# A 4 KB transfer of the first chunk's rows, issued on the ScalarE queue ahead of everything else

## The chip, the core and the metric

The kernel runs on one core of a Trainium2 chip. The metric is the device time of one execution in microseconds, the median of several executions. The profile is of one execution; its span is the time from the core's first to its last instruction.

## What is computed

The input is q, k and v, each of 4 batches, 8 heads, 768 positions and 64 dimensions. Per head there is a retention with a decay of its own, and then a gated feed-forward part over the joined heads:

```python
state = gamma * state + k[t] (outer) v[t]        # per head, 64 x 64
y[t]  = scale * q[t] @ state
x = y with the heads joined: 4 x 768 x 512
h = maximum(x @ w_in, 0)                          # 1024 wide
conv_out = a 3-tap convolution of h along the positions, with conv_w per channel
out = (h * sigmoid(conv_out)) @ w_out             # 512 wide
```

## The kernel before

The retention goes in 24 chunks of 64 positions for two batches at a time. The program on the host has laid q, k (transposed), k and v of one chunk beside each other: `qkv[n]` is 128 rows of 4 slots of 512 floats, so 8 KB a row and 1 MB a chunk. For the first four chunks one load brings slots 0 and 1 (`load`, L348, 4 KB of each row, 512 KB) and a second one slots 2 and 3 (`load_kv`, L352); later chunks come with one load of 1 MB.

The feed-forward part goes in 12 units of 2 x 128 positions. `w_in` and `w_out` arrive as 8-byte numbers, a piece of 512 KB at a time (`load_w`, L476), and VectorE and ScalarE turn each piece into a head and a rest in fp32r (`w_abs` L494 to `w_add` L575). The first product (`mm1`, L589) has the heads and rests of `w_in` (`wi_hi`, `wi_lo`) as the weights of TensorE and `xu` as the moving operand, 256 columns at a time. For six of the units there are combined products (`prod`, L710); some of these use `wi_hi` and `wi_lo` too. The second product (`mm2`, L807) has the gated activations `g` as weights and the converted `w_out`, kept in tiles `h`, as moving operand: 512 columns, and 256 columns for the last tile.

All instructions are given in an order written out by hand (`ORDER`), and every engine works through its own in that order. The beginning is

```
load_w/0 load_w/1 load/0 load_consts load_kv/0 load_w/2 load/1 load_kv/1 load_gy load/2 w_abs/0 ...
... w_head/0 w_clamp/1 w_rest/0 scores/0 w_low/0 masked/0 scale_v/0 w_add/0 w_shift/1 w_abs/2 mix/0
```

All loads are issued on SyncE's queue. TensorE begins with 6 products of zeros (`fill`, L329; each is two passes in the profile), then does `scores/0` (L409), which needs `load/0`, then three more products of zeros (`keep_warm`, L323), and then `mix/0`, which needs the masked scores (`masked`, L436, VectorE) and the scaled v of chunk 0 (`scale_v`, L377, ScalarE, after `load_kv/0`). `load_kv/2` is held back until `mix/0` has been issued.

The SBUF tiles come from two pools, laid out in the order in which the tiles are named. The pool `const` holds 1,664 bytes a partition of constants, then `gy_sb`, `cw_sb`, `wi_hi` (16,384 bytes), a gap of 128, `wi_lo` (16,384), a gap of 128, and, as they are first used, `first` (one float, which takes 32 bytes), `cw_t` (192) and `cw_m` (96). Behind it follows `pool`, whose first tiles are set down by name and size, and then `o_sb` and the chunks `rw`:

```
g_0:4096 g_1:4096 g_2:4096 g_3:4096 h_7:2048 h_8:2048 h_a:2048 h_b:2048 h_e:2048
h_g:2048 h_h:2048 h_k:2048 h_m:2048 h_n:2048 h_q:2048 h_s:2048 h_t:2048 h_1:2080
h_0:2080 h_p:2080 h_3:2080 h_5:2080 h_6:2080 h_j:2080 h_9:2080 h_2:2080 h_c:2080
h_r:2080 h_d:2080 h_f:2080 h_i:2080 h_l:2080 h_o:2080 h_4:2080 h_u:2080 h_v:2080 gap0:32
xu_0:8192 xu_1:8192 xu_2:8192 x_0:2048 ... x_c:2048 m_0:2048 ... cv_2:2048 gap1:64
```

Each DMA counts on one of eight semaphores, taken in turn; a DMA that takes one again waits for the DMA that had it before.

Of the kernel before, what the change touches and what calls it, by code (L numbers as in the profile page):

```python
# [9 lines left out]
F32 = mybir.dt.float32  # L10
# [8 lines left out]
P = 128  # L19
# [244 lines left out]
def retention_then_gated_ffn(  # L264
# [10 lines left out]
    nc = tc.nc  # L275
# [6 lines left out]
    const = ctx.enter_context(tc.tile_pool(name="const", bufs=1))  # L282
# [27 lines left out]
    for i, place_ in enumerate(PLACES.split()):  # L310
        name, size = place_.split(":")
        pool.tile([P, int(size) // 4], F32, name=name, bufs=1)

    warm = pool.tile([P, P], F32, name="o_sb", bufs=2)
    nc.vector.memset(warm, 0.0)
# [570 lines left out]
```

## Time and profile before

| | |
|---|---|
| median of 3 runs | 332.17 us (331.81 to 334.49) |
| the profiled execution | 331.37 us |
| its span | 329.6 us |
| TensorE busy | 319.8 us, 97% of the span |
| VectorE, ScalarE, GpSimd busy | 288.4, 214.8 and 25.7 us |
| read from HBM, written | 33.79 MB, 6.29 MB |
| chain that ended last | TensorE 86%, DMA 6%, VectorE 4% |

The profiled execution took 0.80 us less than the median, and 1.8 us of it lie outside its span. An engine's rows give the start and the duration of an instruction, in microseconds from the start of the span; the bracket behind a row is the idle time of the engine ahead of it and what ended that. A DMA's row is its issue; when its data is there is seen from who starts then.

### The profile page before, as it was taken

To read this page: it belongs to the slowest core of one execution; us is meant where nothing else is said; L and a number is where in the kernel's file an instruction comes from. 1 tells how busy PE (TensorE), PEld (TensorE's weight loads), DVE (VectorE), ACT (ScalarE), POOL (GpSimd) and SP (SyncE) were. 2 spreads that over 40 slices of the span, in tenths; PEclk is the share of its full clock that TensorE was granted. 3 is DMA by queue.
4 is the path that set the end of the run, shared out by engine and by line. 5 is a ranking of instruction groups with operands and counts; after the bars stand their busy time and mean duration, and the time that the engine had idled before them with its cause. 6 is when DMAs were issued, how large, how long until landed. Compare 5 with 4: busy or idle time off the path is not lost.

```text
span 329.6 us, 10762 instructions
## 1 busy us (share of the span) xinstructions
PE 319.8 (97%) x4642; PEld 285.9 (87%) x4642; DVE 288.4 (87%) x566; ACT 214.8 (65%) x448; POOL 25.7 (8%) x100
## 2 busy tenths in 40 slices
PE   8789999999999999999999999999999999999996
PEld 3678999999998988788888998999999888988785
DVE  4699999999999999996999998788988887879980
ACT  4567675747466484855848755976696866676761
POOL 0000002003020200200000000021002200120000
PEclk9999999999999999999999999999999999999999
DMA  6999687736435312463260000000000101010111
GB/s 227 373 337 362 223 286 284 252 133 231 179 132 230 130 57 107 161 233 110 111 195 34 34 0 33 36 0 2 32 34 0 64 2 65 3 64 0 66 64 64
DMA packets 10415, 40.77 MB, mean 124 GB/s; under 512 B 1280, under 2 KB 1792, under 8 KB 7808
## 3 DMA queue, kind: packets, MB, share of 16 engines
q1 hardware_dynamic: 10368, 40.09, 33.6%
q8 instruction: 36, 0.59, 0.7%
q14 instruction: 11, 0.09, 0.1%
HBM read 33.79 MB, written 6.29 MB: 122 GB/s over the span
## 4 chain that ended last, share of the span: by engine, by line
PE 86%; DMA 6%; DVE 4%; ACT 1%; issue 1%; SPq 0%; ACTq 0%
PE ps_o L807 39%; PE ps_m L589 17%; PE ps_m L710 8%; PE ps_y L710 7%; DMA rw<-in_qkv 6%; PE ps_s L409 5%; PE ps_st L409 4%; PE ps_y L409 3%; PE ps_s L710 2%; DVE cv L772 1%; ACT cv L778 1%; PE ps_o L323 0%; DVE cv L783 0%; DVE rw L436 0%; DVE m L512 0%
## 5 line engine op out<-in xcount | busy, mean ns | idle before, releaser
L589 PE MATMUL ps_m<-xu,wi_hi 128*128 128x256 f32 x384 | 68.2, 281 | 0.6 <-ACT h_o L601 0.5
L807 PE MATMUL ps_o<-h,g 128*128 128x512 f32 (+1 forms) x200 | 62.3, 381 | 0.0
L589 PEld LDWEIGHTS ps_m<-xu,wi_hi 128*128 128x128 f32 x384 | 58.0, 188 | 1.9 <-ACT h_o L601 0.7
L589 PE MATMUL ps_m<-xu,wi_lo 128*128 128x256 f32 x192 | 53.2, 277 | 0.0
L778 ACT ACTIVATE cv<-cv 128x512 f32<-128x512 f32 x48 | 29.9, 630 | 34.3 <-DVE cv L772 34.3
L409 PE MATMUL ps_y<-rw 64*64 64x64 f32 x1472 | 48.5, 220 | 0.8 <-issue 0.8
L409 PEld LDWEIGHTS ps_y<-rw 64*64 64x64 f32 x1472 | 45.2, 135 | 1.4 <-issue 0.9
L807 PEld LDWEIGHTS ps_o<-h,g 128*128 128x128 f32 x200 | 37.2, 188 | 6.7 <-ACT o_sb L814 0.2
L772 DVE SCALAR_TENSOR_TENSOR cv<-h,cw_sb,cv 128x256 f32<-128x256 f32 x84 | 38.7, 478 | 1.0 <-ACT cv L767 0.3
L793 DVE TENSOR_TENSOR g<-cv,g 128x512 fp32r<-128x512 f32 x48 | 32.6, 686 | 6.7 <-ACT g L788 6.3
L788 ACT CAST g<-cv 128x512 fp32r<-128x512 f32 x48 | 29.3, 616 | 12.1 <-DVE cv L783 11.0
L589 PEld LDWEIGHTS ps_m<-xu,wi_lo 128*128 128x128 f32 x192 | 36.0, 188 | 0.0
L409 PEld LDWEIGHTS ps_s<-rw 64*64 64x64 f32 x768 | 24.6, 134 | 9.0 <-issue 3.6
L409 PE MATMUL ps_s<-rw 64*64 64x64 f32 x768 | 28.0, 221 | 3.9 <-DMA rw<-in_qkv 1.9
L409 PE MATMUL ps_st<-rw 64*64 64x64 f32 x704 | 24.9, 219 | 0.5 <-ACT rw L377 0.5
L377 ACT ACTIVATE rw<-rw,consts_sb 128x128 f32<-128x128 f32 x64 | 20.4, 390 | 6.4 <-DMA rw<-in_qkv 6.4
L409 PEld LDWEIGHTS ps_st<-rw 64*64 64x64 f32 x704 | 22.6, 135 | 1.5 <-ACT rw L377 0.9
L436 DVE TENSOR_TENSOR rw<-ps_s,consts_sb 128x512 f32<-128x512 f32 x24 | 16.4, 685 | 6.5 <-PE ps_s L409 6.5
L767 ACT ACTIVATE cv<-h,cw_sb 128x256 f32<-128x256 f32 x42 | 20.5, 503 | 2.0 <-DVE g L793 2.0
L814 ACT COPY o_sb<-ps_o 128x512 f32<-128x512 f32 (+1 forms) x25 | 13.9, 560 | 10.1 <-PE ps_o L807 10.0
L807 PE MATMUL ps_o<-h_g,g 128*128 128x512 f32 (+1 forms) x50 | 19.3, 387 | 0.0
L807 PE MATMUL ps_o<-h_s,g 128*128 128x512 f32 (+1 forms) x50 | 19.2, 385 | 0.0
(256 smaller groups left out, 754.6 us busy)
## 6 DMA issues: line engine op xcount, KB each, us to landing
rw<-in_qkv SPq DMA_DIRECT2D x20, 1024.0 KB, 6.0
out_y<-o_sb SPq DMA_DIRECT2D x23, 256.0 KB, 2.2
g<-in_w_in SPq DMA_DIRECT2D x8, 512.0 KB, 5.4
rw<-in_qkv SPq DMA_DIRECT2D x8, 512.0 KB, 7.9
g<-in_w_out SPq DMA_DIRECT2D x8, 512.0 KB, 4.8
out_y<-o_sb SPq DMA_DIRECT2D x2, 128.0 KB, 1.7
consts_sb<-in_consts SPq DMA_DIRECT2D x1, 128.0 KB, 10.2
consts_sb<-in_consts SPq DMA_DIRECT2D x1, 80.0 KB, 7.3
```

Of the source, the lines that this page charges most:

```text
L377: nc.scalar.activation(v[:, :, g], v[:, :, g], AF.Copy, scale=by[:, g : g + 1])
L409: nc.tensor.matmul(out, lhsT, rhs, start=start, stop=stop, skip_group_check=True)
L436: nc.vector.tensor_tensor(out=rw[n][:, 1], in0=s_ps[n], in1=mask_sb.unsqueeze(1).broadcast_to([P, 2, NPAIR, C]), op=ALU.mult)
L589: nc.tensor.matmul(h_ps[u, p][:, odd], w[:, k, fs], x[:, k].rearrange("p b t -> p (b t)"), start=(i == 0), stop=(i == len(products) - 1),)
L710: nc.tensor.matmul(ps[:, i], w[k][:, fs], x[:, k].rearrange("p b t -> p (b t)"), start=(i == m == 0 and q in (1, 5)), stop=(m == len(produ ...
L767: nc.scalar.activation(cvs[u, p][:, i], hs[u, p][:, i, :, 1 : P + 1], AF.Copy, scale=cw_sb[:, f, 1:2])
L772: nc.vector.scalar_tensor_tensor(out=cv, in0=h[:, :, k : k + P], scalar=cw_sb[:, f, k : k + 1], in1=cv, op0=ALU.mult, op1=ALU.add)
L778: nc.scalar.activation(cvs[u, p], cvs[u, p], AF.Sigmoid)
L788: nc.scalar.copy(gs[u, p][:, 0], cvs[u, p])
L793: nc.vector.tensor_tensor(out=lo, in0=cvs[u, p], in1=hi.bitcast(F32), op=ALU.subtract)
L807: nc.tensor.matmul(ps, g, w[f][:, cs], start=(f == 0 and i == 0), stop=(f == NF - 1 and i == 2))
L814: nc.scalar.copy(o[:, :n], o_ps[u, t, h][:, :n])
```

## The change

A tile of 8 floats a partition is added to the pool `const`, ahead of `first`, and ScalarE's first instruction becomes a DMA that brings the first 32 bytes of each of the 128 rows of chunk 0 into it. Nobody reads the tile.

```diff
@@ -311,6 +311,10 @@
         name, size = place_.split(":")
         pool.tile([P, int(size) // 4], F32, name=name, bufs=1)
 
+
+    ahead = const.tile([P, 1, 8], F32, name="ahead")
+    nc.scalar.dma_start(ahead, qkv[0][:, :1, :8])
+
     warm = pool.tile([P, P], F32, name="o_sb", bufs=2)
     nc.vector.memset(warm, 0.0)
     first = const.tile([P, 1], F32, name="first")
```

## Rows read from the trace of the kernel before

**Rows 1.** Page, part 1: busy time of each engine, its share, its instructions.

```profile
PE 319.8 (97%) x4642; PEld 285.9 (87%) x4642; DVE 288.4 (87%) x566; ACT 214.8 (65%) x448; POOL 25.7 (8%) x100
```

**Rows 2.** Chain that ended last, its first 19 us: start, duration, what.

```profile
1.65 7.57 DMA rw<-in_qkv
...
9.25 1.15 PE ps_s L409 x32
10.40 1.49 PE ps_o L323 x6
...
13.07 5.56 DMA rw<-in_qkv
```

**Rows 3.** Windows: length, busy time by engine, clock, DMA share, GB/s.

```profile
2.50:4.50 2.00, 2.00 (x3) 0.67 (x2) 0.00 (x0) 0.47 (x1) 0.00 (x0) 1.00 1.01 403
4.50:7.50 3.00, 3.00 (x8) 1.43 (x7) 2.67 (x6) 1.50 (x3) 0.00 (x0) 1.00 0.78 207
9.00:12.00 3.00, 2.75 (x48) 2.25 (x52) 1.55 (x3) 1.19 (x4) 0.00 (x0) 1.00 1.02 417
14.00:18.00 4.00, 2.77 (x100) 2.28 (x97) 3.43 (x6) 2.51 (x7) 0.00 (x0) 1.00 0.93 314
```

**Rows 4.** Timeline of the first 14 us: ScalarE and SyncE's queue (SPq).

```profile
0.73 1.28 ACT L317 ACT_TABLE_LOAD   x1 [0.73 <-PEq L875]
...
0.74 0.86 SPq L476 DMA_DIRECT2D g<-in_w_in  x2
...
2.03 0.20 ACT L317 ACTIVATE first<-o_sb 128x1 f32<-128x1 f32 x1
...
4.03 0.66 ACT L494 ACTIVATE m<-g 128x512 f32<-128x512 f32 x1 [1.80 <-DMA g<-in_w_in]
4.05 0.58 SPq L352 DMA_DIRECT2D rw<-in_qkv  x1
...
5.31 0.69 ACT L494 ACTIVATE m<-g 128x512 f32<-128x512 f32 x1 [0.61 <-DMA g<-in_w_in]
...
10.81 1.28 ACT L377 ACTIVATE rw<-rw,consts_sb 128x128 f32<-128x128 f32 x4 [3.81 <-DMA rw<-in_qkv]
```

**Rows 5.** Timeline of the first 15 us: TensorE and VectorE.

```profile
1.05 7.27 PE L329 MATMUL ps_o<-o_sb 128*128 128x512 f32 x12 [1.05 <-DVE o_sb L315]
...
7.66 0.68 DVE L528 SCALAR_TENSOR_TENSOR g<-g 128x512 f32<-128x512 uint32 x1
...
10.45 0.69 DVE L436 TENSOR_TENSOR rw<-ps_s,consts_sb 128x512 f32<-128x512 f32 x1 [2.11 <-PE ps_s L409]
...
14.61 0.69 DVE L436 TENSOR_TENSOR rw<-ps_s,consts_sb 128x512 f32<-128x512 f32 x1 [0.57 <-PE ps_s L409]
```

**Rows 6.** DMA issues: KB of each, median microseconds from issue to landing.

```profile
rw<-in_qkv SPq DMA_DIRECT2D x8, 512.0 KB, 7.9
```

**Rows 7.** Groups of TensorE's instructions by form: count, busy, mean ns, idle before.

```profile
L589 PE MATMUL ps_m<-xu,wi_hi 128*128 128x256 f32 x384 | 68.2, 281 | 0.6 <-ACT h_o L601 0.5
...
L589 PE MATMUL ps_m<-xu,wi_lo 128*128 128x256 f32 x192 | 53.2, 277 | 0.0
...
L710 PE MATMUL ps_m<-xu,wi_hi 128*128 128x256 f32 x48 | 8.7, 281 | 0.0
...
L710 PE MATMUL ps_m<-xu,wi_lo 128*128 128x256 f32 x24 | 6.6, 276 | 0.0
```

**Rows 8.** Timeline of TensorE in two stretches: 211 to 215 us, and 324 to 326 us.

```profile
211.07 0.39 PE L710 MATMUL ps_m<-xu,wi_hi 128*128 128x256 f32 x2
...
213.80 0.39 PE L807 MATMUL ps_o<-h,g 128*128 128x512 f32 x1
...
215.17 1.53 PE L710 MATMUL ps_y<-xu,rw 128*128 128x256 f32 x12
...
324.02 0.28 PE L807 MATMUL ps_o<-h_b,g 128*128 128x256 f32 x1
...
325.94 0.28 PE L807 MATMUL ps_o<-h_s,g 128*128 128x256 f32 x1
```

## The prediction

> **What bounds the kernel now.** First the page: TensorE is busy 97% of the span [rows 1], so a gain has to begin in TensorE's idle time or shorten its instructions. The chain of waits says where the idle time is: of its first 19 us 7.57 + 5.56 = 13.13 are two DMAs of `qkv` [rows 2], the first of them `load/0`, issued at 1.65 and followed at 9.25 by `scores/0`. The change touches this one.
>
> The windows show why `load/0` is late. The queue works in order: `load_w/0`, `load_w/1`, `load/0`. The two pieces of `w_in` flow at 403 GB/s and are there when ScalarE starts on them, at 4.03 and 5.31 [rows 3, 4]: 1.28 us for 512 KB. The next 512 KB are `load/0` [rows 6], and they would be there at 5.31 + 1.28 = 6.6. They land at 1.65 + 7.57 = 9.22, since between 4.5 and 7.5 us only 207 GB/s flow, with the DMA engines 78% busy [rows 3]. From 9 to 12 us, where the same queue brings chunk 1 from the neighbouring megabyte among other things, it is 417 GB/s again. The transfer added reads rows of chunk 0 before its turn; if the slow stretch belongs to the first reading of that memory, some of it could pass while `w_in` flows.
>
> **What late data costs.** Not all of the 2.6 us can come back. The products of zeros end at 1.05 + 7.27 = 8.32 [rows 5], and `scores/0` stands behind them: it can start 9.25 - 8.32 = 0.93 us earlier and no more. Then TensorE goes on without idle time into `keep_warm` and `mix/0` (9.25 + 1.15 = 10.40, + 1.49 = 11.89 [rows 2]), so 0.93 is the cap there too, if the v of chunk 0 is scaled in time: ScalarE waits for `load_kv/0` until 10.81 [rows 4], and that transfer stands behind `load/0` and moves with it. `load_kv/2`, held by `mix/0` and issued at 13.07, moves as well. VectorE is idle for 2.11 us ahead of the first `masked`, and 0.57 us ahead of the second, at 14.61 [rows 5]; from there on to the end of the 30 us its row of instructions has no idle time that the timeline marks. So what the start can give in all is 0.93, or 0.93 + 0.57 = 1.50 if that second hole closes too.
>
> **The change part by part.**
>
> *The issue on ScalarE.* The trace has no DMA issue on that engine. SyncE's cost 0.43 (0.86 for two) to 0.58 [rows 4], and I take 0.5. ScalarE's table load and the first activation end at 2.03 + 0.20 = 2.23; they would end at 2.73. The next instruction waits for `load_w/0` until 4.03 [rows 4]. Cover 1.80, cost on the path nothing; without the cover 0.5.
>
> *The packets.* 128 rows of 32 bytes, 4 KB. From below the time is that of 4 KB at 403 GB/s, 0.01 us; from above that of a transfer with as many rows of 4 KB, 1.28 [rows 4]. It is nearer to the lower end by bytes, and I take 0.1. If all of the 1.28 were put ahead of `load_w/0`, VectorE's conversions, which end at 7.66 + 0.68 = 8.34 [rows 5], would end at 9.6, and `load/0` without its slow stretch would land at 6.6 + 1.28 = 7.9, still before 8.32. So this too is covered where the transfer helps; where it doesn't, `scores/0` is late by 0.1, at most 1.28.
>
> *The semaphore.* The new DMA takes the first of the eight, so the ninth, `load_kv/1`, has to wait for it. SyncE issues that at 4.05 [rows 4], by when `load_w/0`, issued beside the new one, has landed (4.03). Behind it are `load_gy` and `load/2`. Cost nothing; all other pairs that share a semaphore keep their distance of eight.
>
> *The gain.* Between 0 and 0.93. For a gain: chunk 1 is read without a slow stretch, so rows, size and pitch alone don't make one. Against: the windows of 14 to 18 us, with `load/2` and `load_kv/2`, flow at 314 GB/s with the engines 93% busy [rows 3], so reading `qkv` is slowed elsewhere too, by something that 32 bytes a row may not take away. I take the middle, 0.5.
>
> The Trainium skill, in its page HBM Reference, section Latency, gives 0.2 us for an access on average and 2 us under high load. By that rule load makes reading slow, and the touch would gain nothing: 332.2 instead of 331.7. The trace disagrees: the higher rate goes with the faster stretch [rows 3].
>
> *The 32 bytes.* The tile `ahead` stands in the pool `const` behind `wi_hi` and `wi_lo` and moves all of `pool` up by 32 bytes a partition. The weights of L589 and of some of L710 stay, and their moving operand moves. By the sizes in the code `xu` begins 33,344 (`wi_hi` to the end of `const`) + 16,384 (`g`) + 26,624 + 39,520 (`h`) + 32 = 115,904 bytes above `wi_hi`, 192 past a multiple of 256, and 64 past one above `wi_lo`; with the change 224 and 96. Does this matter? Two stretches of products with 256 columns differ: 24 of L710 take 213.80 - 211.07 = 2.73 us, 114 ns each, and 16 of L807 take 325.94 - 324.02 = 1.92, 120 ns each [rows 8]. In L807 weights `g` and moving `h` are a multiple of 256 apart. With 512 columns L807 takes (215.17 - 213.80) / 6 = 228 ns [rows 8], so there nothing is seen of it. That the distance is the cause is my reading. Distances of 224 and 96 have no row: 114 ns is one bound, 120 the other. From below no row of 256 columns is faster than 114, and I leave a small chance that one would be. The products concerned are 384 + 192 of L589 and three times 48 + 24 of L710 (the two rows shown and two pairs alike) [rows 7], 792 in all; times 6.2 ns that is 0 to 4.9 us, nearly all on the path with TensorE 97% busy. I take 0, the row of the same instructions, and keep the other end for the range.
>
> **The sum.** 331.37 - 0.5 = 330.9 for the profiled execution, which was 0.80 below the median; on the scale of the median 332.17 - 0.5 = 331.7.
>
> **The rivals.**
>
> *Slower: the products with `wi_hi` and `wi_lo` lose their distance.* For it: the 120 against 114 ns, and 792 products on the engine that is the bound. Against: with a distance between the two seen, part or none of it may come. Half gives 331.7 + 2.5 = 334.2, all 336.6. It decides from 0.5 / 792 = 0.6 ns a product upwards, and is over 1% from (335.5 - 331.7) / 792 = 4.8 ns, a pace of 119.
>
> *The touch doesn't do what it is for.* The slow stretch stays: rows are slow one by one, or because 16 engines read `qkv` in step. Then 332.2, and up to 332.3 with the packets in the way. For it the 314 GB/s at 14 to 18 us, against it the 417 at 9 to 12 [rows 3].
>
> *More than the cap at `scores/0`.* If the second hole of VectorE closes too: 332.17 - 1.5 = 330.7. Against it: VectorE has no idle time to give back afterwards.
>
> **How the numbers follow.** The forecast, a gain of 0 to 0.93 with the pace unchanged, 331.2 to 332.2: 0.42. The slower pace: 0.33, of which 0.13 over 335.5. The touch without effect: 0.17. The larger gain: 0.05. A faster pace: 0.03. The range goes from 330.4, the larger gain with 0.3 for the runs' own scatter (332.17 - 331.81 = 0.36), to 335.5, where 0.13 is left out above and some 0.04 below. One per cent, 3.3 us, is about what a measurement of this kernel can tell from no change. Over 1% faster needs the faster pace: 0.03. Over 1% slower: 0.13. Within: 0.84.
>
> **What would show it.** `scores/0` starts at 8.3 to 8.8 instead of 9.25, and the window of 4.5 to 7.5 us flows at more than 300 GB/s: the touch works. If that window stays near 207 and `scores/0` at 9.25 or later, it doesn't. The start of `mix/0`, 11.89 before, shows what is passed on; if `load_kv/2` is issued earlier and VectorE's masking at 14.61 is not, it was lost there. 24 products of L710 at about 211 us in 2.73 us: the pace is kept; in 2.8 or more: the 32 bytes cost. The prediction is wrong if the pace changes, or if `load_w/0` is delayed by more than the 1.8 us of cover.

## The result and the profile after

The changed kernel takes 334.11 us (median of 22 runs, 332.52 to 337.97), the kernel before 331.70 beside it (22 runs, 330.43 to 335.34). The ratio is 1.0062, with an interval of 1.0039 to 1.0085: slower by 0.6%, some 2 us. The ratio goes by the mean and leaves out one slow execution; the medians of all lie 2.4 us apart. 331.7 had been forecast. The profiled executions lie 334.87 - 331.37 = 3.5 us apart, and their spans 333.1 - 329.6 = 3.5.

The change adds four lines, so L589, L710 and L807 of before are L593, L714 and L811 here. The page, part 1, which answers to [rows 1]:

```profile
PE 323.9 (97%) x4642; PEld 289.6 (87%) x4642; DVE 288.6 (87%) x566; ACT 214.8 (65%) x448; POOL 25.7 (8%) x100
```

TensorE has the same 4642 products and is busy 4.1 us longer; the others work as long as before, within 0.2 us. So the time was not lost in a wait. The groups by form, against [rows 7], say which products have become longer (count, busy, mean ns of one):

```profile
L593 PE MATMUL ps_m<-xu,wi_hi 128*128 128x256 f32 x384 | 70.6, 285 | 0.1
L593 PE MATMUL ps_m<-xu,wi_lo 128*128 128x256 f32 x192 | 53.9, 280 | 0.0
...
L714 PE MATMUL ps_m<-xu,wi_hi 128*128 128x256 f32 x48 | 9.0, 285 | 0.0
...
L714 PE MATMUL ps_m<-xu,wi_lo 128*128 128x256 f32 x24 | 6.7, 281 | 0.0
```

281 has become 285, and 277 or 276 has become 280 or 281. These durations overlap, so the pace is read from start to start. The chain of waits has unbroken runs of such products; first before, then after:

```profile
51.74 7.05 PE ps_m L589 x60
61.82 7.03 PE ps_m L589 x60
...
211.23 2.72 PE ps_m L710 x24
```

```profile
51.60 7.29 PE ps_m L593 x60
63.02 7.33 PE ps_m L593 x60
...
214.05 2.84 PE ps_m L714 x24
```

60 products take 0.24 to 0.30 us more, 4 to 5 ns each. (The length of such a run includes the whole of its last product, so it is more than 60 times the pace.) The 24 products that the prediction named, in TensorE's timeline, with the row that follows them (against [rows 8]):

```profile
213.89 0.40 PE L714 MATMUL ps_m<-xu,wi_hi 128*128 128x256 f32 x2
214.13 0.28 PE L714 MATMUL ps_m<-xu,wi_lo 128*128 128x256 f32 x1
...
216.38 0.39 PE L714 MATMUL ps_m<-rw,wi_hi 128*128 128x256 f32 x2
216.61 0.28 PE L714 MATMUL ps_m<-rw,wi_lo 128*128 128x256 f32 x1
216.73 0.40 PE L811 MATMUL ps_o<-h,g 128*128 128x512 f32 x1
```

216.73 - 213.89 = 2.84 us for 24, 118 ns each, where it was 2.73 and 114. With 792 products of this kind and 4 to 5 ns that is 3.2 to 4.0 us. The intervals from each of TensorE's products to the next, compared one by one with before's, give it by line, where no gap lies between them: 2.4 us more on L593, 1.1 on L714, 0.5 on L811. These are 3.9 us together; 0.3 of them were given back at the start, and about as much in seven longer gaps on L811.

The start, in the windows that answer to [rows 3] (length, busy time of PE, PEld, DVE, ACT, POOL, then clock, DMA share, GB/s):

```profile
2.50:4.50 2.00, 2.00 (x3) 0.67 (x2) 0.00 (x0) 0.40 (x2) 0.00 (x0) 1.00 0.96 364
4.50:7.50 3.00, 3.00 (x6) 1.25 (x5) 2.44 (x6) 1.71 (x3) 0.00 (x0) 1.00 0.85 267
...
14.00:18.00 4.00, 3.49 (x128) 3.16 (x128) 4.00 (x7) 2.70 (x9) 0.00 (x0) 1.00 1.00 307
```

and in the timeline, against [rows 4, 5]:

```profile
0.73 0.40 ACTq L316 DMA_DIRECT2D ahead<-in_qkv  x1
...
1.05 7.95 PE L333 MATMUL ps_o<-o_sb 128*128 128x512 f32 x12 [1.05 <-DVE o_sb L319]
1.16 1.28 ACT L321 ACT_TABLE_LOAD   x1 [1.16 <-PEq L879]
...
2.46 0.20 ACT L321 ACTIVATE first<-o_sb 128x1 f32<-128x1 f32 x1
...
4.26 0.66 ACT L498 ACTIVATE m<-g 128x512 f32<-128x512 f32 x1 [1.60 <-DMA g<-in_w_in]
4.42 0.33 SPq L356 DMA_DIRECT2D rw<-in_qkv  x1
...
8.93 1.15 PE L413 MATMUL ps_s<-rw 64*64 64x64 f32 x32
9.58 1.28 ACT L381 ACTIVATE rw<-rw,consts_sb 128x128 f32<-128x128 f32 x4 [2.36 <-DMA rw<-in_qkv]
```

The issue costs ScalarE 0.40 us, and 1.60 of its wait for `load_w/0` are left. `scores/0` starts 0.32 us earlier, at 8.93, and its row names no wait for a DMA any more: it follows the products of zeros, which end at 9.00 in this execution (8.32 before). So the data came earlier and the work in front of it ended later. The window of 4.5 to 7.5 us has 267 GB/s where it had 207, which is neither the more than 300 nor the 207 that the prediction named as its signs, and that of 14 to 18 us, of which the prediction said that the touch may not help it, 307 where it had 314.

### The profile page after: what moved, and what is told of

Read it like the earlier page. It is cut to its first block, busy times and chain, and to the rows that moved or that the text cites. A ratio compares the mean times of both kernels' runs of the same rounds, so it can differ in the third digit from the quotient of the medians.

```text
span 333.1 us, 10763 instructions
## 1 busy us (share of the span) xinstructions
PE 323.9 (97%) x4642; PEld 289.6 (87%) x4642; DVE 288.6 (87%) x566; ACT 214.8 (65%) x448; POOL 25.7 (8%) x100
## 4 chain that ended last, share of the span: by engine, by line
PE 95%; DVE 2%; issue 1%; ACT 0%; ACTq 0%; DVEq 0%
PE ps_o L811 40%; PE ps_m L593 21%; PE ps_m L714 8%; PE ps_y L714 7%; PE ps_s L413 6%; PE ps_st L413 5%; PE ps_y L413 3%; PE ps_s L714 3%; PE ps_o L333 2%; DVE rw L440 0%; DVE m L516 0%; DVE x L454 0%; DVE gy_sb L371 0%; DVE wi_lo L579 0%; DVE g L532 0%
## 5 line engine op out<-in xcount | busy, mean ns | idle before, releaser
L593 PE MATMUL ps_m<-xu,wi_hi 128*128 128x256 f32 x384 | 70.6, 285 | 0.1
L811 PE MATMUL ps_o<-h,g 128*128 128x512 f32 (+1 forms) x200 | 62.5, 382 | 0.0
L593 PEld LDWEIGHTS ps_m<-xu,wi_hi 128*128 128x128 f32 x384 | 58.9, 188 | 1.3 <-issue 0.3
L593 PE MATMUL ps_m<-xu,wi_lo 128*128 128x256 f32 x192 | 53.9, 280 | 0.0
L811 PEld LDWEIGHTS ps_o<-h,g 128*128 128x128 f32 x200 | 37.2, 188 | 6.9 <-ACT o_sb L818 0.2
L593 PEld LDWEIGHTS ps_m<-xu,wi_lo 128*128 128x128 f32 x192 | 36.1, 188 | 0.0
L811 PE MATMUL ps_o<-h_s,g 128*128 128x512 f32 (+1 forms) x50 | 19.2, 386 | 0.0
L811 PE MATMUL ps_o<-h_g,g 128*128 128x512 f32 (+1 forms) x50 | 19.1, 385 | 0.0
```

Source lines behind the costliest of these rows:

```text
L593: nc.tensor.matmul(h_ps[u, p][:, odd], w[:, k, fs], x[:, k].rearrange("p b t -> p (b t)"), start=(i == 0), stop=(i == len(products) - 1),)
L811: nc.tensor.matmul(ps, g, w[f][:, cs], start=(f == 0 and i == 0), stop=(f == NF - 1 and i == 2))
```

## Experiments

The theory: the distance in SBUF between a product's weights and its moving operand, modulo 256 bytes, sets the pace of the products with 256 columns. `xu` stands 192 bytes past a multiple of 256 above `wi_hi` and 64 past one above `wi_lo`; with the change 224 and 96. The first rival: it is the transfer that costs. The second: it is the alignment of the moved tiles by itself. The third question is what the touch gives at the start.

### The transfer alone: touch_only

The 32 bytes go into the gap of 128 behind `wi_lo`, and no tile moves.

```diff
-    const.tile([P, LOWER], F32, name="gap_3")
+    gap_3 = const.tile([P, LOWER], F32, name="gap_3")
+    nc.scalar.dma_start(gap_3[:, :8].unsqueeze(1), qkv[0][:, :1, :8])
```

> The transfer alone: it lands in the first 32 bytes of the gap behind wi_lo, and no tile moves. Theory A (the 32 bytes cost the pace of the products with wi_hi and wi_lo, the transfer itself gains a little): 0.3 to 1.0 us faster than before (ratio 0.997 to 0.999), the products of L589 at 113 to 114 ns as before, load/0 landing at about 7.8 instead of 9.2. Theory B (the transfer itself, its queue or its packets make the kernel slower): ratio about 1.006, as with the whole change.

Measured: 331.68 us against 331.46, ratio 1.0003 (0.998 to 1.0027); the 0.3 to 1.0 us that were expected are not seen. The chain's runs of products keep their pace:

```profile
50.44 7.05 PE ps_m L590 x60
...
209.56 2.72 PE ps_m L711 x24
```

The transfer costs nothing that can be measured, and gives nothing that can be.

### The 32 bytes alone: shift_32

```diff
+    const.tile([P, 8], F32, name="ahead")
     warm = pool.tile([P, P], F32, name="o_sb", bufs=2)
```

> The tile alone, without the transfer: pool moves up by 32 bytes. Theory A: about 3 us slower than before (ratio 1.008 to 1.010), with 24 products of L710 with wi_hi and wi_lo in 2.8 us or more, and load/0 landing at 9.2 as before. Theory B: ratio 1.000.

Measured: 334.57 us against 331.46, ratio 1.0095 (1.0063 to 1.0126).

```profile
52.90 7.29 PE ps_m L590 x60
...
214.09 2.84 PE ps_m L711 x24
```

A tile that nothing writes or reads makes the kernel slower, at the pace of the changed kernel. The first rival falls. One expectation was missed: by the semaphore events of this trace `load/0` lands at 7.70 us, and not at 9.2, without any transfer ahead of it.

### Other distances: shift_64, shift_128, minus_32

As shift_32, with a tile of 16 floats, and of 32; and the kernel before with the 32 bytes of `gap0` taken out of the list of places, so that `xu` and all behind it moves down.

```diff
+    const.tile([P, 16], F32, name="ahead")
```

```diff
+    const.tile([P, 32], F32, name="ahead")
```

```diff
-h_r:2080 h_d:2080 h_f:2080 h_i:2080 h_l:2080 h_o:2080 h_4:2080 h_u:2080 h_v:2080 gap0:32
+h_r:2080 h_d:2080 h_f:2080 h_i:2080 h_l:2080 h_o:2080 h_4:2080 h_u:2080 h_v:2080
```

> A tile of 64 bytes without a transfer: xu then begins a multiple of 256 above wi_hi and 128 past one above wi_lo. Theory A, by the 120 ns of the last tile of L807, whose weights and moving operand are a multiple of 256 apart: 528 products with wi_hi at 120 and 264 with wi_lo at 117 to 120, 4 to 5 us slower than before (ratio 1.012 to 1.015). Rival C (what counts is a start that isn't a multiple of 64 bytes apart, so 32 is worst and 64 is as good as before): ratio 1.000.

> A tile of 128 bytes without a transfer: xu begins 64 past a multiple of 256 above wi_hi and 192 above wi_lo, the two distances of the kernel before with their places changed. Theory A (the distance between weights and moving operand, not the place of pool): ratio 1.000, products of L589 at 113 to 114 ns. Rival D (any move of pool out of the place for which it was laid out costs): slower, as with 32 bytes.

> The kernel before with the same gap taken out and nothing added: xu and what lies behind it move down by 32 bytes, g and h stay. Theory A: as slow as the 32 bytes upwards, ratio 1.007 to 1.011, with the products of L589 at 116 to 120 ns. A rival by which only a move upwards or the place of g and h costs: ratio 1.000.

Measured: shift_64 1.009 (1.0058 to 1.0122), shift_128 1.0044 (1.0018 to 1.007), minus_32 1.0066 (1.0034 to 1.0098). Chains of shift_64, shift_128 and minus_32, in this order:

```profile
51.63 7.34 PE ps_m L590 x60
```

```profile
53.08 7.32 PE ps_m L590 x60
...
213.40 2.72 PE ps_m L711 x24
```

```profile
51.67 7.26 PE ps_m L589 x60
```

With 64 bytes the alignment to 64 is what it was, and the products are slow all the same: the second rival falls for multiples of 64. By the pace the loss is the one that was expected from L807's 120 ns: the products start 119 ns apart on average, which makes 4 us on L590 and L711 in this trace. In the times 3.0 us of it are left (1.9 to 4.0, four runs), where 4 to 5 had been expected. shift_128 was expected to cost nothing and missed that: by the distances `wi_hi` and `wi_lo` exchange their places, 64 and 192, and some runs of products are slow (the one of 60), others not (the one of 24), about half of all; on L590 it is 1.2 us in all, where shift_32 lost 2.5. So the plain form of the theory, by which 64 and 192 are good wherever they stand, is not right.

### The same distances at other addresses: swap_128

128 bytes more, and `wi_lo` allocated ahead of `wi_hi`. Every tile of `pool` moves by 128 and both weights move, but the distances are 192 and 64 again, each with its own tile.

```diff
-    wi_hi = const.tile([P, NPAIR, DFF], F32R, name="wi_hi")
-    const.tile([P, LOWER], F32, name="gap_2")
...
+    const.tile([P, LOWER], F32, name="gap_2")
+    wi_hi = const.tile([P, NPAIR, DFF], F32R, name="wi_hi")
...
+    const.tile([P, 32], F32, name="ahead")
```

> The 128 bytes of the run before it, and wi_lo laid down ahead of wi_hi: the distance of xu from wi_hi and from wi_lo is then the one of the kernel before for each of the two (192 and 64 past a multiple of 256). If the distance from each, taken modulo 256, decides: ratio 1.000 and 113 to 114 ns, so 128 bytes cost 0.4% only because the two had changed places. If something else of the place counts: the 0.4% stay.

Measured: 1.0012 (0.9981 to 1.0043), and the pace of before:

```profile
51.17 7.05 PE ps_m L590 x60
...
210.37 2.72 PE ps_m L711 x24
```

Against shift_128 only the order of the two weights differs, so it is not the address of `pool`; and move_xu, below, loses the pace with both weights in place. What is left is where weights and moving operand stand to each other. That the period is 256 bytes is supported by the same two runs: in swap_128 `xu` is 16,384 bytes nearer to `wi_hi` and 16,640 further from `wi_lo`, 64 and 65 times 256, and the pace is kept; in shift_128 it is 128 further from both, and part of the pace is lost.

### Which of the moved tiles: refit, move_xu, move_g_h

refit is the change with `gap0` taken out: `xu` and all behind it are where they were, `g` and `h` remain 32 bytes up. move_g_h is the same without the transfer. move_xu moves `xu`, `x`, `m` and `cv` alone.

The first diff is common to refit, where the lines of the change stand beside it, and move_g_h, where an empty tile of 8 floats does; the second is move_xu.

```diff
-h_r:2080 h_d:2080 h_f:2080 h_i:2080 h_l:2080 h_o:2080 h_4:2080 h_u:2080 h_v:2080 gap0:32
+h_r:2080 h_d:2080 h_f:2080 h_i:2080 h_l:2080 h_o:2080 h_4:2080 h_u:2080 h_v:2080
```

```diff
-h_r:2080 h_d:2080 h_f:2080 h_i:2080 h_l:2080 h_o:2080 h_4:2080 h_u:2080 h_v:2080 gap0:32
+h_r:2080 h_d:2080 h_f:2080 h_i:2080 h_l:2080 h_o:2080 h_4:2080 h_u:2080 h_v:2080 gap0:64
...
-x_6:2048 x_7:2048 x_8:2048 x_9:2048 x_a:2048 x_b:2048 x_c:2048 m_0:2048 m_1:2048 m_2:2048 cv_0:2048 cv_1:2048 cv_2:2048 gap1:64
+x_6:2048 x_7:2048 x_8:2048 x_9:2048 x_a:2048 x_b:2048 x_c:2048 m_0:2048 m_1:2048 m_2:2048 cv_0:2048 cv_1:2048 cv_2:2048 gap1:32
```

> The whole change with the gap of 32 bytes ahead of xu taken out: transfer and tile stay, g and h move up by 32 bytes, but xu, the tiles behind it and rw lie where they lay before. Theory A (the distance between wi_hi or wi_lo and xu costs): back to the kernel before (ratio 0.998 to 1.002), L589's and L710's products with wi_hi and wi_lo at 113 to 114 ns; only 72 products of L710 with xu and the h tiles change their distance, 0.3 us. Rival B (the transfer or the moved pool): ratio stays near 1.006.

> The kernel before with 32 bytes of the gap behind cv moved ahead of xu: only xu, x, m and cv lie 32 bytes higher; wi_hi, wi_lo, g, h and rw stay. Theory A (the distance between weights and moving operand): as slow as the tile of 32 bytes or slower, ratio 1.008 to 1.013, since besides the products with wi_hi and wi_lo those of L710 with rw and h as weights lose their distance from xu too (another 288). A rival by which the place of the whole pool costs: ratio near 1.000.

> The tile of 32 bytes without the transfer, and the gap ahead of xu taken out: only g and h (with first, cw_t and cw_m) lie 32 bytes higher than before. In the run with the transfer this was 0.5% slower. If that came from the place of g and h: 1.0 to 1.6 us slower again (ratio 1.003 to 1.005), with the products of L807 losing about 0.8 us and those of L710 with h 0.3. If it came from the transfer or from the executions' scatter: ratio 0.999 to 1.002.

Measured: move_xu 1.0105 (1.0061 to 1.0149), the whole loss of shift_32 with a fraction of its tiles. refit 1.0048 (1.0021 to 1.0076), where no difference was expected; move_g_h 1.0004 (0.997 to 1.0038). In the profiled execution of move_xu the granted clock is 0.50 from 46.4 to 49.8 us, so of its trace only the pace outside that stretch is used. It holds a comparison of its own, since products with the same weights have their moving operand either in `xu`, which has moved, or in `rw`, which has not. First two groups by form, then the timeline where the one kind goes over into the other:

```profile
L710 PE MATMUL ps_m<-xu,wi_lo 128*128 128x256 f32 x24 | 6.7, 280 | 0.0
...
L710 PE MATMUL ps_m<-rw,wi_lo 128*128 128x256 f32 x24 | 6.6, 277 | 0.0
```

```profile
219.28 0.39 PE L710 MATMUL ps_m<-xu,wi_hi 128*128 128x256 f32 x2
...
220.35 0.40 PE L710 MATMUL ps_m<-rw,wi_hi 128*128 128x256 f32 x2
...
221.38 0.39 PE L710 MATMUL ps_m<-rw,wi_hi 128*128 128x256 f32 x2
```

The ones with `rw` keep the 276 to 277 ns of before, the ones with `xu` have the 280 to 281 of after [rows 7]. From start to start nine products with `xu` take 220.35 - 219.28 = 1.07 us, 119 ns each, and the nine with `rw` right behind them 1.03, 114 each. Chains of move_xu and refit:

```profile
57.60 7.29 PE ps_m L589 x60
```

```profile
52.30 7.05 PE ps_m L593 x60
...
212.26 2.73 PE ps_m L714 x24
...
283.73 2.81 PE ps_y L714 x24
```

With `xu` back in its place the pace is back. The last line shows products that in refit have become slow instead: they have `h` as weights and `xu` as moving operand, 24 in 2.81 us where before, after and touch_only have 2.73. There `h` has moved and `xu` has not. That makes some 0.2 us of refit's 1.6; L811 took another 0.8 between its unbroken products in its trace and in that of move_g_h. Since move_g_h has the same places, refit's remainder is not explained by them.

### The start: before_again, fill_4, fill_4_touch

The kernel before once more, unchanged; then 4 products of zeros instead of 6 ahead of `scores/0` (two are left out, no output depends on them), without and with the transfer into the gap.

```diff
-FILL = 6
+FILL = 4
```

> The kernel before once more, unchanged, for a second profile of its start. If the slow stretch of load/0 to 9.2 us belongs to the kernel without the transfer: load/0 lands at about 9 again. If it was a matter of that one execution: at 7.6 to 7.9, as in the three runs with a tile and no transfer, and scores/0 starts where the products of zeros end.

> The kernel before with 4 products of zeros at the beginning instead of 6. In ten profiles the products of zeros end between 7.9 and 9.4 us, in nine of them at or after the landing of load/0 (7.6 to 8.3). If they set the start of scores/0: it starts at the landing of load/0, 0.3 to 1 us earlier, ratio 0.997 to 1.000. Rival: the granted clock rises later when TensorE has less to do ahead of it, and the gain is lost.

> The same with the transfer into the gap behind wi_lo. With 4 products of zeros the landing of load/0 is uncovered. If the transfer shortens the slow stretch at all, scores/0 starts earlier than in the run without it and the ratio is 0.5 to 1 us lower; if it does nothing, load/0 lands at 7.6 to 8.3 in both and the two ratios agree within 0.002.

Measured: before_again 332.06 us. In the window of 4.5 to 7.5 us it has 309 GB/s, not 207, and its `scores/0` waits for no DMA:

```profile
4.50:7.50 3.00, 3.00 (x6) 1.35 (x5) 1.95 (x5) 1.74 (x3) 0.00 (x0) 1.00 0.94 309
```

```profile
1.05 8.18 PE L329 MATMUL ps_o<-o_sb 128*128 128x512 f32 x12 [1.05 <-DVE o_sb L315]
9.16 1.03 PE L409 MATMUL ps_s<-rw 64*64 64x64 f32 x28
```

The late landing is not confined to one execution, though: in the trace of move_g_h, also without the transfer, `scores/0` waits for `load/0` again.

```profile
9.09 1.15 PE L410 MATMUL ps_s<-rw 64*64 64x64 f32 x32 [0.86 <-DMA rw<-in_qkv]
```

fill_4 took 1.0028 (1.0002 to 1.0055), where 0.997 to 1.000 was expected, and fill_4_touch 0.9999 (0.9973 to 1.0025). With the fill out of the way the wait for `load/0` shows, first without and then with the transfer:

```profile
8.87 1.15 PE L409 MATMUL ps_s<-rw 64*64 64x64 f32 x32 [1.43 <-DMA rw<-in_qkv]
```

```profile
7.83 1.15 PE L410 MATMUL ps_s<-rw 64*64 64x64 f32 x32 [0.72 <-DMA rw<-in_qkv]
```

One execution each, and `scores/0` comes 1.04 us earlier with the transfer; in the times the two differ by 0.0029, with intervals that overlap. By the semaphore events of all fourteen traces `load/0` lands at 7.8 to 8.3 us in the four with the transfer; in the ten without it lands at 7.6 to 8.2 in seven, and at 8.8 to 9.2 in before, move_g_h and fill_4. Four traces without a late landing against three late ones in ten show nothing of the transfer. The loads of 512 KB have a median from issue to landing of 6.6, 6.6, 7.0 and 6.6 us in the four traces with the transfer, and of 6.3 to 7.9 in the ten without, seven of these at 6.9 or less. Nor do the times agree on a sign where the transfer is all that differs: the changed kernel lies 0.0033 below shift_32, fill_4_touch 0.0029 below fill_4, touch_only 0.0003 above before, refit 0.0044 above move_g_h. A small gain is possible, and not shown.

## Why the prediction failed, step by step

**The 32 bytes: the step that failed.** The prediction counted the right 792 products, named the cause to look at, gave bounds of 114 and 120 ns, and then took 0, "the row of the same instructions". That row was taken at the old distance, which is just what the edit changes, so it was no evidence for the new one. Measured are 118 ns, two thirds of the way to the upper bound: 3.4 us in the trace (L593 and L714), 2 us in the times of the whole change and 3 in those of shift_32. The rival was the right one in kind. That its price at half, 334.2, meets the 334.11 so closely is luck: the pace lost two thirds and not half, the gain of 0.5 in that sum was not seen, and the kernel before took 331.70 beside it and not 332.17. touch_only and shift_32 show that the transfer is not the cause; swap_128 and move_xu show that the distance is, and shift_128 that its plain form is not yet the whole rule.

**The gain of 0.5: mis-sized, from one execution.** The 207 GB/s of [rows 3] and the wait of 0.93 ahead of `scores/0` did not belong to the kernel: before_again has 309 GB/s and no such wait. Among the ten traces without the transfer that window has 207 to 315 GB/s, among the four with it 267 to 299, so one trace could not tell a gain. What sets `scores/0` there, as in the changed kernel, is the end of the products of zeros. touch_only gives 1.0003 where 0.5 us would be 0.9985; its interval allows 0.7 us of gain and 0.9 of loss. So nothing here speaks against the rival "the touch doesn't do what it is for", and none of its reasons is shown.

**The cap.** The prediction took 8.32 for the end of the products of zeros as if it were fixed. It varies, with the same instructions, from 7.88 (touch_only) to 9.47 (shift_128); what goes with it is shown at the end. So `scores/0` could neither be expected at 8.3 to 8.8 nor was a later start a sign against the touch.

**What held.** The issue on ScalarE: 0.40 us where 0.5 was taken, under a cover of which 1.60 is left. The view named as a test, 24 products in 2.8 us or more, decided it. The semaphore: `load_kv/1` does wait for the transfer, which takes 3.7 us to land, so that it is issued at 4.42 and not at 4.05:

```profile
ahead<-in_qkv ACTq DMA_DIRECT2D x1, 4.0 KB, 3.7
```

This costs nothing, as forecast though not for the reason given: the loads ahead of it in the queue land until 12.06.

**What can't be told.** The packets: `load_w/0` is used 0.23 us later (4.26 against 4.03), within the bounds of 0.01 to 1.28 and covered, but in the ten traces without the transfer it lands anywhere from 4.0 to 4.7, so the 0.23 can't be put down to them. The second hole of VectorE: it has closed, against the forecast, with the second masking at 13.63 and no idle time ahead of it, but it has closed in before_again too (13.86), without the transfer; no gain from it is seen in the times.

**What stays open.** Why 64 and 192 are good with one weight tile and not with the other (shift_128). Why L811 takes 0.3 to 0.8 us more between its unbroken products in most kernels with moved tiles, where its two operands moved together or, in minus_32, not at all (0.5). Why the changed kernel lost only 2 us in the times, where its pace lost 3.4 in the trace and shift_32 lost 3 in the times; the intervals of the two ratios overlap. Whether refit's 0.5% is real, as move_g_h didn't show it. Whether the touch gives some tenths. And what slows the stretch of 4.5 to 7.5 us in some executions.

Nothing tried is faster than the kernel before. Whoever wants the touch puts it into the gap that is there: touch_only costs nothing that was measured.

## What to carry to other kernels

A tile added to a pool moves everything that is laid down behind it; before an edit is costed at its instructions, ask which matmul operands change their place relative to each other, and compare the pace of a long unbroken run in the chain of waits. A row measured under the condition that the edit removes is no reason to take the lower bound. A wait at the start that one trace shows should be seen in a second trace before a gain is taken from it.

## What the runs showed of the hardware

The pace of products with 256 columns goes with the distance between weights and moving operand. The `xu` column is the bytes past a multiple of 256 above `wi_hi` and `wi_lo`, by the sizes in the code; the pace is the mean from start to start on the first product (L589, L590 or L593), with `wi_hi` and with `wi_lo` as weights, gaps left out.

| kernel | `xu` above `wi_hi`, `wi_lo` | ns a product, `wi_hi`, `wi_lo` | ratio |
|---|---|---|---|
| before, touch_only, swap_128 | 192, 64 | 114, 114 | -, 1.0003, 1.0012 |
| after, shift_32, move_xu | 224, 96 | 118 to 119, 118 | 1.0062, 1.0095, 1.0105 |
| shift_64 | 0, 128 | 119, 119 | 1.009 |
| minus_32 | 160, 32 | 119, 116 | 1.0066 |
| shift_128 | 64, 192 | 116, 116 (half 113 to 114, half 117 to 124) | 1.0044 |

With 512 columns the median is 227 ns in every kernel. That says little of the distance: these products are all L807's, whose operands `g` and `h` stand a multiple of 256 apart in every run. Whether it is the load of the weights or the stream of the moving operand that is held up, the runs don't tell. The Trainium skill, in its page TensorE: Matmul & The Clock Gate, section Back-to-back issue gap, gives the isolated gap between two products by the number of columns and the clock alone (262 cycles for 256 columns, 109 ns at 2.4 GHz), and says that in a stream of weight loads and products both set the spacing. No run here is as fast as the isolated gap, and at one number of columns and one granted clock, 1.00, the mean is 114 to 119 ns by the place of the tiles.

The products of zeros start slowly and come to double pace at a time that differs from one execution to the next. The weight loads ahead of each pass, of the kernel before, of before_again and of touch_only (start, duration, and the idle time ahead):

```profile
4.63 0.29 PEld L329 LDWEIGHTS ps_o<-o_sb 128*128 128x128 f32 x1 [0.52 <-issue]
5.16 0.19 PEld L329 LDWEIGHTS ps_o<-o_sb 128*128 128x128 f32 x1 [0.24 <-issue]
```

```profile
6.34 0.34 PEld L329 LDWEIGHTS ps_o<-o_sb 128*128 128x128 f32 x1 [0.52 <-issue]
6.92 0.19 PEld L329 LDWEIGHTS ps_o<-o_sb 128*128 128x128 f32 x1 [0.25 <-issue]
```

```profile
3.77 0.27 PEld L330 LDWEIGHTS ps_o<-o_sb 128*128 128x128 f32 x1 [0.52 <-issue]
4.29 0.19 PEld L330 LDWEIGHTS ps_o<-o_sb 128*128 128x128 f32 x1 [0.24 <-issue]
```

The passes before the first of these rows start 0.85 us apart and those behind the second 0.43, a ratio of two, as between TensorE's levels of 1.2 and 2.4 GHz. The windows give a granted clock of 1.00 in all of this stretch, but also where the trace has no entry of it. The trace's own entries of the granted clock begin at 4.82 us in the kernel before, at 6.64 in before_again and at 3.94 in touch_only, each with 1.00, and in all fourteen traces the first entry, between 3.94 and 7.12 us, falls where the passes change their spacing. So the step goes with the granted clock; that the stretch ahead of it ran at the lower level is read from the ratio. The step alone moves the end of 12 equal passes by some 1.6 us from trace to trace, as much as the effects that were looked for at the start.
